# Sketched attention and a rational MoE layer on one core: the last tokens leave PSUM in two column halves

## The chip, the cores and the metric

The kernel runs on one core of one Trainium2 chip, as one program. The time is the device time of one execution in microseconds; the medians here are over repeated runs of the same program. Beside that, one execution was recorded by the hardware profiler; all rows quoted below come from that one, and their times count from the first instruction of its span.

A core has five engines that matter here: TensorE (PE in the profile, with its weight loads as PEld), VectorE (DVE), ScalarE (ACT), GpSimd (POOL) and SyncE (SP), which mostly issues transfers. SP and ScalarE each have a queue of their own for transfers (q1 and q10 in the profile), and the transfers are carried out by 16 DMA engines.

## The reference: what is computed

Four batches of four heads, 1,088 tokens each, head size 32. Queries and keys go through two small sketches, whose outer product gives 64 features per token; from these a linear attention is computed. Its output, 4,352 tokens of 128 numbers, goes through a layer of 2,048 hidden units with a rational activation:

```python
def phi(x):
    a = np.einsum('rd,bhsd->bhsr', S1, x)
    b = np.einsum('rd,bhsd->bhsr', S2, x)
    return np.einsum('bhsi,bhsj->bhsij', a, b).reshape(*x.shape[:-1], r * r)
q_p, k_p = (phi(q), phi(k))
kv = np.einsum('bhsf,bhsd->bhfd', k_p, v)
num = np.einsum('bhsf,bhfd->bhsd', q_p, kv)
den = np.einsum('bhsf,bhf->bhs', q_p, np.sum(k_p, axis=2))[..., None] + 1e-06
...
h = x @ w_in
P = a[0] + a[1] * h + a[2] * h2 + a[3] * h3
Q = 1.0 + np.abs(b[0]) * np.abs(h) + np.abs(b[1]) * h2
out = (P / (Q + 1e-06)) @ w_out
```

The result is 4,352 x 128 in float32, token by token: batch b has rows b x 1,088 to b x 1,088 + 1,087.

## The kernel before, in words

Of each batch 1,024 tokens are cut into two chunks of 512, the first chunk of all into 128 and 384. The 64 tokens that each batch has left over, 4 x 64 = 256, form one last chunk, number 9. Each chunk goes through the same steps: the attention gives its tokens, transposed, in the tile xT; the 16 blocks of the hidden layer (128 units each) are multiplied in groups, the activation is computed on VectorE and ScalarE with some sums done by accumulating transfers from GpSimd's queue, and the products with w_out are summed in one PSUM tile, out_ps (`project`).

For chunks 0 to 8 the sum stands there with the model dimension on the partitions; it is copied to SBUF, transposed by TensorE, copied by ScalarE into the tile oT (`oT_evac`, L906) and stored by SP (`store_main`, L981). The last chunk is summed by token (`BY_TOKEN`): its matmuls (L886) take 128 tokens as the weights, so out_ps has tokens on the partitions and no transpose is needed. Columns 0 to 127 of out_ps hold the left-over tokens of batches 0 and 1 (64 partitions each), columns 128 to 255 those of batches 2 and 3. One copy by ScalarE (`o_tokens`, L962) brings all 256 columns to oT, and `store_rem` (L985 to L989) issues two stores, one on SP's and one on ScalarE's queue: store i takes the partitions 64 i to 64 i + 63 with both column halves, that is the batches i and i + 2.

The kernel lists its steps through `plan.add`, each with an engine, an estimated length, the steps that it follows and the buffers that it takes and gives. The order in which the steps are issued is not planned at run time: the list `ORDER` at the head names the steps by number, and `Plan.issue` runs through it. Each engine works through its instructions in that order and waits for the others by counters; which waits an instruction gets follows from the tiles that it reads and writes. The stores of all chunks go through a tile oT with two buffers.

Of the kernel before, what the change touches and what calls it, by code (L numbers as in the profile page):

```python
# [15 lines left out]
ACT = mybir.ActivationFunctionType  # L16
# [39 lines left out]


class Plan:
# [66 lines left out]
def kernel(  # L125
# [13 lines left out]
    nc = tc.nc  # L139
    B, H, S, D = q.shape  # L140
    R = S1.shape[0]
    n_tok, d_model = out.shape
# [4 lines left out]
    MAIN = J * 128  # L147
    REM = S - MAIN
# [7 lines left out]
    BP = B // 2  # L156
# [26 lines left out]
    plan = Plan(BUFS)  # L183
    T = {}

    def tile_of(pool, name, shape, dtype):
        return pool.tile(shape, dtype, name=name, bufs=BUFS[name])
# [45 lines left out]
    def load_small(eng, i):  # L233
        s = (S1, S2)[i]
        QUEUE[eng].dma_start(out=SR[:, i, :],
                             in_=bass.AP(tensor=s.tensor, offset=s.offset, ap=[[0, 128 // R], [D, R], [1, D]]))

    def load_ab(eng):
        for dst, src in ((b_sb, moe_b), (a_sb, moe_a)):
            QUEUE[eng].dma_start(out=dst, in_=bass.AP(tensor=src.tensor, offset=src.offset,  # L240
                                                      ap=[[0, 128]] + list(src.ap)))
# [34 lines left out]
    i = plan.add("POOL", 1500, lambda: load_small("POOL", 1), rank=-99.9, name="load S2")  # L276
# [20 lines left out]
    for b in range(2, B):  # L297
        for i, (name, go) in enumerate(mains(b)):
            ld[name, b] = load("SP", go, 512, NP if name == "v" else 1, rank=-70 + i,
                               take=["v_aug" if name == "v" else "kq"])  # L300
# [69 lines left out]
    i = plan.add("POOL", 1350, lambda: load_ab("POOL"), after=[c_pool], rank=-98.9, name="load ab")  # L370
# [235 lines left out]
    def lab(n):  # L606
        return n - 1 if n > 1 else ("0", "0b")[n]
# [179 lines left out]
    def add_group(g, G):  # L787
        W, fis, n, how = G["W"], G["fis"], G["n"], G["how"]
# [26 lines left out]
        def take(kind):  # L815
            return [] if packed else [KINDS[kind][0]]

        def got(kind):
            return [T[kind, "got", n]] if packed else []

        def used(step, *kinds):
            if packed:
                for kind in kinds:
                    T[kind, "used", n].append(step)
            return step

        def give(*kinds):
            return [] if packed else [KINDS[kind][0] for kind in kinds]
# [41 lines left out]
        def mul(out, in0, in1):  # L870
            return lambda: nc.vector.tensor_mul(out=out(), in0=in0(), in1=in1())  # L871
# [38 lines left out]
        for s, nsub in subs:  # L910
            at = s * W // CW if W > B * REM or not by_token else s
            hm = plan.add("PE", 858 * nsub * W // 512, lambda s=s, w=nsub: h_mm(s, w), after=[G["x_step"], ld["wi"]], rank=g - 1.45,
                          take=["h_ps"], give=["xT"] if final and (s, nsub) == subs[-1] else [], name=f"h {g},{at}")
# [3 lines left out]
                                take=take("t") if s == 0 else [], give=["h_ps"], name=f"hev {g},{at}"))  # L917
# [3 lines left out]
        def add_up(name, dst, src, after, rank, give=()):  # L921
            if name[1] not in how:
                return plan.add("DVE", tt, lambda: nc.vector.tensor_add(out=dst(), in0=dst(), in1=src()), after=after,
                                rank=rank, give=give, name=f"{name} {g}")

            def f():
                nc.gpsimd.dma_start(out=dst(), in_=src(), accum_op=AX.add, max_dma_last_dim=GW)  # L927
            p = plan.add("POOL", 1900, f, after=after, rank=rank, name=f"{name} {g}")
            return plan.add("DMA", -(-gw // 2048) * 2048 * 1.43 if gw > 1024 else gw * 1.43, lambda: None, after=[p], rank=rank, give=give, lag=900, name=f"{name} land {g}")
# [10 lines left out]
        p = plan.add("DVE", ts + 121, odd, after=[sp, c_a] + got("y"), rank=g - 0.3, take=take("y"), name=f"odd {g}")  # L940
        p = used(plan.add("DVE", tt, mul(y, y, ht), after=[p, ab], rank=g - 0.3, give=give("t"), name=f"oddt {g}"), "t")
# [3 lines left out]
        if z:  # L945
            rt = plan.add("PE", len(fis) * pw, lambda: project("u", w_out_0, first, False),
                          after=[e, rt] + c_w0[:1 + (fis[-1] >= NF // 2)], rank=g + 0.45, take=["out_ps"] if first else [], name=f"pr {g}")
            used(rt, "u")
        p = used(add_up("+P", y, sq, [p, v, dq0], g - 0.3, give=give("sq")), "sq")
        p = used(plan.add("DVE", tt, mul(y, y, u), after=[p, e], rank=g + 0.55, give=[] if z else give("u"), name=f"n5 {g}"), "u")  # L950
        o = plan.add("PE", len(fis) * pw, lambda: project("y", w_out_b, first and not z, final), after=[p, rt] + c_w[:1 + (fis[-1] >= NF // 2)], rank=g + 0.56,
                     take=["out_ps"] if first and not z else [], give=give("y"), name=f"py {g}")
# [6 lines left out]
        if final and by_token:  # L959
            def o_tokens():  # L960
                T["oT", n] = tile_of(moe, "oT", [128, JC, d_model], FP)
                nc.scalar.copy(out=T["oT", n][:, :W // 128, :],  # L962
                               in_=T["o", n][:, :W].rearrange("p (n d) -> p n d", d=d_model))

            t = plan.add("ACT", 32 + W * 109 // 128, o_tokens, after=[o], rank=g + 0.57, take=["oT"], give=["out_ps"],
                         name=f"otev {lab(n)}")
            t = plan.add("SP", 650, lambda: G["store"](T["oT", n]), after=[t], rank=g + 0.6, name=f"store {lab(n)}")
            plan.add("ST", 1, lambda: None, after=[t], rank=g + 0.6, give=["oT"], name=f"stored {lab(n)}")
        elif final:
            ev = 32 + W * 109 // 128  # L970
            o = plan.add("ACT", ev, o_evac, after=[o], rank=g + 0.56, take=["o_sb"], give=["out_ps"], name=f"oev {lab(n)}")
            t = plan.add("PE", 110 * (W // 128), o_transposes, after=[o], rank=g + 0.57, take=["w_ps"], give=["o_sb"],
                         name=f"otr {lab(n)}")
            t = plan.add("ACT", ev, oT_evac, after=[t], rank=g + 0.57, take=["oT"], give=["w_ps"], name=f"otev {lab(n)}")
            t = plan.add("SP", 650, lambda: G["store"](T["oT", n]), after=[t], rank=g + 0.6, name=f"store {lab(n)}")
            plan.add("ST", 1, lambda: None, after=[t], rank=g + 0.6, give=["oT"], lag=700, name=f"stored {lab(n)}")
        return o

    def store_main(b, c, j0, nj):
        def f(oT):  # L980
            nc.sync.dma_start(  # L981
                out=out[b * S:b * S + MAIN, :].rearrange("(p j) d -> p j d", j=J)[:, c * JC + j0:c * JC + j0 + nj, :], in_=oT[:, :nj])
        return f

    def store_rem(oT):  # L985
        for i, eng in enumerate((nc.sync, nc.scalar)):
            eng.dma_start(out=bass.AP(tensor=out.tensor, offset=out.offset + (i * S + MAIN) * d_model,
                                      ap=[[d_model, REM], [2 * S * d_model, BP], [1, d_model]]),
                          in_=oT[i * REM:(i + 1) * REM, :BP, :])  # L989

    chunks = [(b, c, 0, JC) for b in range(B) for c in range(NCH)]
    chunks[0:1] = [(0, 0, 0, HEAD), (0, 0, HEAD, JC - HEAD)]
# [2 lines left out]
    for n in range(len(chunks) + 1):  # L995
# [4 lines left out]
        for z in sizes:  # L1000
            groups.append(dict(n=n, W=B * REM if rem else chunks[n][3] * 128, fis=list(range(f0, f0 + z)),
                               store=store_rem if rem else store_main(*chunks[n])))
# [6 lines left out]
    for n in range(len(chunks) + 1):  # L1009

        rank = first_of[n] - 2.6
        if n < len(chunks):
# [5 lines left out]
            def srcs(b=b, c=c, j0=j0, nj=nj):  # L1018
# [13 lines left out]
                give=["kq"] if c == NCH - 1 else [], early=early, pair=c if b > 0 else None)  # L1032
# [57 lines left out]
```

## Time and profile before

| what | us |
|---|---|
| median of 3 runs | 246.57 (246.38 to 246.75) |
| the profiled execution | 246.79 |
| its span, first to last instruction | 244.8 |
| busy in the span: PE, DVE, ACT | 237.0, 223.8, 219.4 |
| last copy out of PSUM (L962) | 0.37, from 240.86 |
| last two stores (L987) issued | 241.26 |

The page of the profile gives busy times of each engine, the chain of work that ended last (followed back from the last instruction: what released it, and what released that), and groups of instructions by line. The timeline lists instructions with their start and length; `<-PE out_ps` in brackets says what ended the wait before one. The DMA view lists, for a stretch of time, the share of the 16 DMA engines that were busy in 40 equal slices (a digit is tenths, 9 is 90% or more), the packets of each queue with the share of the stretch that they took on 16 engines, and the transfers issued in it with size and time from issue to landing.

### The profile page before, as it was taken

Reading aid. Unit: us, or ns where it says so; the run is one execution under the profiler, and the core shown is the slowest. Engines: PE = TensorE matmul, PEld = TensorE weight load, DVE = VectorE, ACT = ScalarE, POOL = GpSimd, SP = SyncE. Lnnn points to the kernel's source line nnn. Section 1 sums busy time; section 2 is a strip of 40 time slices with the busy share of each in tenths; the row PEclk is TensorE's granted clock in tenths of the full one; section 3 lists DMA queues with packets and bytes.
Section 4 is the critical chain, followed back from the end, with each engine's and each line's share of the span. In section 5 each row is a group of like instructions: output and inputs, shape, how many; then the busy total and the mean of one; then the engine's idle time right before and its main releaser. Section 6 shows DMA issues by size and latency. Waiting matters only on the chain.

```text
span 244.8 us, 3043 instructions
## 1 busy us (share of the span) xinstructions
PE 237.0 (97%) x1138; PEld 137.0 (56%) x1138; DVE 223.8 (91%) x241; ACT 219.4 (90%) x198; POOL 50.1 (20%) x70
## 2 busy tenths in 40 slices
PE   8999999999999999999999999999999999999983
PEld 4888676655566555554554655344344444655452
DVE  0759969999999999999999999999999998999992
ACT  3337998998899979999999999999999999999993
POOL 7800020104021505030121420212211113111100
PEclk9999999999999999999999999999999999999999
DMA  6996716668959799989999899999999999999912
GB/s 165 277 319 170 255 22 111 166 135 196 188 99 185 126 183 181 188 158 191 205 173 184 151 212 187 187 209 183 189 189 215 185 175 181 203 190 179 194 43 67
DMA packets 22207, 42.96 MB, mean 175 GB/s; under 512 B 5537, under 2 KB 12721, under 8 KB 22065
## 3 DMA queue, kind: packets, MB, share of 16 engines
q0 software_dynamic: 8544, 31.74, 72.5%
q1 hardware_dynamic: 13360, 10.95, 14.9%
q8 instruction: 9, 0.15, 0.2%
q10 hardware_dynamic: 288, 0.08, 0.2%
q14 instruction: 6, 0.04, 0.0%
HBM read 8.82 MB, written 2.23 MB: 45 GB/s over the span
## 4 chain that ended last, share of the span: by engine, by line
PE 81%; DVE 8%; DMA 4%; ACT 4%; issue 2%; SPq 0%; DVEq 0%; ACTq 0%
PE h_ps L834 44%; PE out_ps L891 11%; PE w_ps L501 7%; DVE y L871 4%; PE w_ps L688 3%; PE w_ps L630 3%; PE w_ps L464 3%; PE w_ps L676 3%; DMA u<-lin 3%; PE w_ps L620 2%; ACT L L875 2%; DMA kq<-in_k_dram 2%; ACT u L878 2%; PE w_ps L455 1%; DVE lin L861 1%
## 5 line engine op out<-in xcount | busy, mean ns | idle before, releaser
L834 PE MATMUL h_ps<-xT,w_in_sb 128*128 128x512 f32 (+3 forms) x320 | 127.4, 534 | 0.0
L834 PEld LDWEIGHTS h_ps<-xT,w_in_sb 128*128 128x128 f32 x320 | 55.2, 190 | 42.1 <-issue 32.4
L875 ACT ACTIVATE L<-u,kappa 128x4096 f32<-128x4096 bf16 (+6 forms) x23 | 65.9, 2866 | 0.2 <-DMA u<-lin 0.2
L878 ACT ACTIVATE u<-L 128x4096 bf16<-128x4096 f32 (+6 forms) x23 | 63.7, 2769 | 0.1
L841 ACT CAST hb<-h_ps 128x1024 bf16<-128x1024 f32 (+3 forms) x52 | 52.1, 1022 | 5.1 <-PE h_ps L834 4.9
L927 POOL DMA_DIRECT2D u<-lin x17 | 21.1, 1241 | 115.8 <-DVE u L853 42.2
L871 DVE TENSOR_TENSOR y<-y,u 128x4096 bf16<-128x4096 bf16 (+6 forms) x23 | 39.6, 1727 | 1.1 <-ACT u L878 1.1
L871 DVE TENSOR_TENSOR y<-y,hb 128x4096 bf16<-128x4096 bf16 (+6 forms) x23 | 39.6, 1728 | 0.1
L861 DVE TENSOR_TENSOR lin<-hb 128x4096 bf16<-128x4096 bf16 (+6 forms) x22 | 38.0, 1728 | 0.7 <-ACT hb L841 0.6
L927 POOL DMA_DIRECT2D y<-lin x15 | 20.6, 1370 | 61.6 <-DVE lin L868 19.8
L891 PE MATMUL out_ps<-y,w_out_b 128*128 128x512 bf16 (+2 forms) x144 | 30.6, 355 | 0.9 <-DVE y L871 0.9
L865 DVE TENSOR_SCALAR y<-lin,a_t 128x4096 bf16<-128x4096 bf16 (+6 forms) x23 | 25.0, 1089 | 1.1 <-PE out_ps L891 0.9
L891 PEld LDWEIGHTS <-w_out_b 128*128 128x128 bf16 x144 | 13.3, 98 | 20.2 <-issue 7.9
L853 DVE TENSOR_SCALAR u<-hb 128x4096 int16<-128x4096 int16 (+6 forms) x23 | 21.6, 941 | 0.3 <-ACT hb L841 0.2
L891 PE MATMUL out_ps<-u,w_out 128*128 128x512 bf16 x64 | 15.1, 379 | 0.0
L841 DVE CAST hb<-h_ps 128x1024 bf16<-128x1024 f32 x12 | 14.6, 1214 | 0.0
L501 PEld LDWEIGHTS w_ps<-v_aug,k_p 128*128 128x128 f32 x112 | 13.4, 192 | 1.3 <-issue 1.0
L501 PE MATMUL w_ps<-v_aug,k_p 128*128 128x96 f32 x112 | 13.7, 274 | 0.0
L484 DVE TENSOR_TENSOR k_p<-ab 128x1024 f32<-128x1024 f32 x7 | 8.6, 1231 | 3.9 <-ACT q_pT L682 2.3
L891 PEld LDWEIGHTS <-w_out 128*128 128x128 bf16 x64 | 6.2, 98 | 8.4 <-issue 2.3
L868 DVE TENSOR_SCALAR lin<-lin,a_t 128x4096 bf16<-128x4096 bf16 (+3 forms) x11 | 10.9, 989 | 0.0
L676 PEld LDWEIGHTS w_ps<-ident,q_p 128*128 128x128 f32 x66 | 8.1, 141 | 5.0 <-issue 4.6
(121 smaller groups left out, 230.5 us busy)
## 6 DMA issues: line engine op xcount, KB each, us to landing
u<-lin POOLq DMA_DIRECT2D x14, 1024.0 KB, 9.4
y<-lin POOLq DMA_DIRECT2D x13, 1024.0 KB, 9.8
v_aug<-in_v_dram SPq DMA_DIRECT2D x8, 256.0 KB, 5.0
out_dram<-oT SPq DMA_DIRECT2D x7, 256.0 KB, 4.7
kq<-in_k_dram SPq DMA_DIRECT2D x3, 512.0 KB, 4.3
kq<-in_q_dram SPq DMA_DIRECT2D x3, 512.0 KB, 6.3
u<-lin POOLq DMA_DIRECT2D x2, 768.0 KB, 8.0
w_in_sb<-in_moe_w_in_dram SPq DMA_DIRECT2D x1, 1024.0 KB, 5.6
```

The source lines that it names most:

```text
L501: nc.tensor.matmul(kv_of((hp,))[:, 0], lhsT=lhs(hp), rhs=rhs(hp), start=(first and hp == hps[0]), stop=final, skip_group_check=True)
L676: nc.tensor.transpose(T["qpTp", n, hp][:, i * 128:(i + 1) * 128], in_=qp[:, i, hp * 128:(hp + 1) * 128], identity=ident)
L834: nc.tensor.matmul(T["h", g, s][:, i * step:i * step + W], lhsT=w_in_sb[:, fi * 128:(fi + 1) * 128], rhs=T["xT", n][:, :W], start=True, st ...
L841: copy(out=T["t", g][:, s * W:(s + nsub) * W], in_=T["h", g, s][:, :nsub * W])
L853: nc.vector.tensor_scalar(out=u().bitcast(mybir.dt.int16), in0=ht().bitcast(mybir.dt.int16), scalar1=0x7FFF, scalar2=None, op0=AX.bitwise_and)
L861: nc.vector.tensor_mul(out=sq(), in0=ht(), in1=ht())
L865: nc.vector.tensor_scalar(out=y(), in0=sq(), scalar1=a_t[:, 3:4], scalar2=a_t[:, 1:2], op0=AX.mult, op1=AX.add)
L871: return lambda: nc.vector.tensor_mul(out=out(), in0=in0(), in1=in1())
L875: nc.scalar.activation(out=T["L", g][:, :gw], in_=u(), func=ACT.Ln, bias=1.0 + 1e-6, scale=kappa[:, 2:3])
L878: nc.scalar.activation(out=u(), in_=T["L", g][:, :gw], func=ACT.Exp, scale=-1.0)
L891: nc.tensor.matmul(T["o", n][:, :W], lhsT=w[:, fi, :], rhs=T[src, g][:, i * W:(i + 1) * W], start=(start and i == 0), stop=(stop and i == ...
L927: nc.gpsimd.dma_start(out=dst(), in_=src(), accum_op=AX.add, max_dma_last_dim=GW)
```

## The change

The 256 columns of the last chunk are copied out of PSUM by two engines: columns 0 to 127 by ScalarE, columns 128 to 255 by VectorE. The two stores are divided the same way: SP stores the first half (batches 0 and 1, all 128 partitions), ScalarE's queue the second (batches 2 and 3). One step more is in the plan, so the numbers behind it rise by one, and the new step (800) stands right behind ScalarE's copy (799) in the order.

```diff
-     794, 798, 792, 679, 780, 790, 795, 793, 799, 796, 731, 800, 732, 801, 797]
+     794, 798, 792, 679, 780, 790, 795, 793, 799, 800, 796, 731, 801, 732, 802, 797]
...
             def o_tokens():
                 T["oT", n] = tile_of(moe, "oT", [128, JC, d_model], FP)
-                nc.scalar.copy(out=T["oT", n][:, :W // 128, :],
-                               in_=T["o", n][:, :W].rearrange("p (n d) -> p n d", d=d_model))
-
-            t = plan.add("ACT", 32 + W * 109 // 128, o_tokens, after=[o], rank=g + 0.57, take=["oT"], give=["out_ps"],
-                         name=f"otev {lab(n)}")
-            t = plan.add("SP", 650, lambda: G["store"](T["oT", n]), after=[t], rank=g + 0.6, name=f"store {lab(n)}")
+                nc.scalar.copy(out=T["oT", n][:, :W // 256, :],
+                               in_=T["o", n][:, :W // 2].rearrange("p (n d) -> p n d", d=d_model))
+
+            def o_batches():
+                nc.vector.tensor_copy(out=T["oT", n][:, W // 256:W // 128, :],
+                                      in_=T["o", n][:, W // 2:W].rearrange("p (n d) -> p n d", d=d_model))
+
+            t = plan.add("ACT", 32 + W * 109 // 256, o_tokens, after=[o], rank=g + 0.57, take=["oT"], name=f"otev {lab(n)}")
+            t2 = plan.add("DVE", 72 + W // 2, o_batches, after=[o], rank=g + 0.57, give=["out_ps"], name=f"otev2 {lab(n)}")
+            t = plan.add("SP", 650, lambda: G["store"](T["oT", n]), after=[t, t2], rank=g + 0.6, name=f"store {lab(n)}")
...
     def store_rem(oT):
-        for i, eng in enumerate((nc.sync, nc.scalar)):
-            eng.dma_start(out=bass.AP(tensor=out.tensor, offset=out.offset + (i * S + MAIN) * d_model,
-                                      ap=[[d_model, REM], [2 * S * d_model, BP], [1, d_model]]),
-                          in_=oT[i * REM:(i + 1) * REM, :BP, :])
+        for k, eng in enumerate((nc.sync, nc.scalar)):
+            eng.dma_start(out=bass.AP(tensor=out.tensor, offset=out.offset + (2 * k * S + MAIN) * d_model,
+                                      ap=[[S * d_model, 2], [d_model, REM], [1, d_model]]), in_=oT[:, k])
```

The list in `ap` gives step and count of each dimension of the DRAM side, outermost first: before 64 rows, 2 batches, 128 numbers; after 2 batches, 64 rows, 128 numbers. On the side of SBUF the partitions are outermost: 64 before, 128 after.

14 rows, old and new, of the table ORDER are left out of this document.

## The prediction

> **What bounds the kernel now.** I read the page first: its busy times, and the shares of the chain that ended last.
>
> ```profile
> span 244.8 us, 3043 instructions
> ...
> PE 237.0 (97%) x1138; PEld 137.0 (56%) x1138; DVE 223.8 (91%) x241; ACT 219.4 (90%) x198; POOL 50.1 (20%) x70
> ...
> PE 81%; DVE 8%; DMA 4%; ACT 4%; issue 2%; SPq 0%; DVEq 0%; ACTq 0%
> ```
>
> Three engines are busy nine tenths of the span, and TensorE carries 81% of the chain. None of that is touched: up to the last matmul both kernels issue the same instructions in the same order on every engine. So the question is only what follows that matmul. The timeline of the end:
>
> ```profile
> 240.19 0.29 DVE L871 TENSOR_TENSOR y<-y,u 128x256 bf16<-128x256 bf16 x1 [0.29 <-ACT u L878]
> 240.54 0.28 PE L886 MATMUL out_ps<-w_out_b,y 128*128 128x128 bf16 x2
> 240.66 0.33 SPq L981 DMA_DIRECT2D out_dram<-oT  x1
> 240.86 0.37 ACT L962 COPY oT<-out_ps 128x256 f32<-128x256 f32 x1 [0.23 <-PE out_ps L886]
> 241.26 0.65 SPq L987 DMA_DIRECT2D out_dram<-oT  x1
> 241.26 0.69 ACTq L987 DMA_DIRECT2D out_dram<-oT  x1
> ```
>
> The last copy runs from 240.86 to 241.23, and the two last stores are issued 0.03 us later, together. Next the DMA view of 241.2 to 244.9 (the digits are the busy share of the 16 DMA engines in slices of 0.0925 us):
>
> ```profile
> DMA  0006999999600016999996100000000000000000
> ...
> DMA packets 432, 0.39 MB, mean 106 GB/s; under 512 B 48, under 2 KB 304, under 8 KB 432
> ...
> out_dram<-oT SPq DMA_DIRECT2D x1, 64.0 KB, 2.1
> out_dram<-oT ACTq DMA_DIRECT2D x1, 64.0 KB, 2.4
> ```
>
> Three stores fall in it, each of 144 packets (432/3): 128 of data and 16 of less than 512 B, the number of DMA engines. The digits 9 say that nearly all engines work at once. ScalarE's store lands last, at 241.26 + 2.4 = 243.66; from there to the end of the span are 244.8 - 243.66 = 1.14 us, which I keep. So the end is: copy 0.37, hop 0.03, store 2.4, closing 1.14. All the change can win by quicker copies is a few tenths; what a store costs is the large term.
>
> **The change, part by part.**
>
> *The copies.* ScalarE copies 128 columns instead of 256, VectorE the other 128:
>
> ```profile
> L896 ACT COPY o_sb<-out_ps 128x128 f32<-128x128 f32 x1 | 0.3, 277 | 0.0
> L721 DVE TENSOR_TENSOR o_sb<-w_ps,den_e 128x128 f32<-128x128 f32 x1 | 0.3, 281 | 0.0
> L566 DVE TENSOR_TENSOR z_bd<-w_ps,mask 128x16 f32<-128x16 f32 x2 | 0.3, 168 | 0.0
> ```
>
> ScalarE: 0.28 for 0.37, so SP's store can be issued at 240.86 + 0.28 + 0.03 = 241.17, 0.09 earlier. VectorE's copy has no row. By the 128x128 multiply out of PSUM it is 0.28; the 128x16 row bounds it below at 0.17. I take 0.28. But the two do not run side by side. They write one tile, oT, and in the changed program the last wait of VectorE's copy is for ScalarE's counter at the value of ScalarE's copy. VectorE answers ScalarE within 0.03 us (its 240.19 above, after a ScalarE instruction that ran from 239.74 for 0.42):
>
> ```profile
> 239.74 0.42 ACT L878 ACTIVATE u<-L 128x256 bf16<-128x256 f32 x1
> ```
>
> So it copies from 241.17 to 241.45, and ScalarE's store is issued at 241.48, 0.22 later than now. Behind that wait ScalarE has nothing but the end of the program; behind the copy VectorE has nothing. VectorE's copy also waits for earlier stores out of the same buffer. The youngest of them was issued at 236.40 and took 4.2, so it is in at 240.6, before the last matmul ends, and costs nothing:
>
> ```profile
> 236.40 0.33 SPq L981 DMA_DIRECT2D out_dram<-oT  x1
> ```
>
> ```profile
> out_dram<-oT SPq DMA_DIRECT2D x1, 256.0 KB, 4.2
> ```
>
> *The stores.* Before, store i takes 64 partitions and two batches: 64 x 2 runs of 128 floats, and the outermost dimension is 64 in SBUF and 64 in DRAM. After, store k takes all 128 partitions of one half: 128 runs in SBUF, but 2 (batches) x 64 x 128 in DRAM. Runs, bytes and their length (512 B) stay; what changes is that the DRAM side's outermost dimension falls from 64 to 2. That matters if a store is dealt out to the DMA engines by its outermost dimension. What the rows say for it: the shape goes to the queue with its dimensions, since the issue of the two-dimensional stores takes 0.65 and 0.69, that of the plain one 0.33; and a store whose two sides both begin with 64 uses all sixteen engines. With 128 on one side and 2 on the other, the only equal cut that fits both outermost dimensions is in two. No store or load of the trace has a dimension below 16 outermost, so it cannot show the case itself; the bounds are sixteen engines (nothing changes) and two.
>
> The Trainium skill, page "DMA: Bandwidth & Descriptors", section "Why a DMA increments its semaphore by 16 and not by 1", states the rule outright: the engine count is the largest number up to 16 that divides the outermost dimension of both patterns, and the lowest-numbered engines are taken. By it each of these stores gets two engines, and both stores the same two. The trace agrees for 64 (16 small packets a store); no run here shows a 2.
>
> The price by rows. One packet of 512 B, from a dense stretch of the first loads (2.6 to 3.0, all packets of 512 B), from the last two stores (242.45 to 243.45), from the first of these while crowded (242.45 to 242.86), and packets of 2,048 B of the store before them (241.2 to 242.4):
>
> ```profile
> DMA packets 255, 0.13 MB, mean 326 GB/s; under 512 B 0, under 2 KB 255, under 8 KB 255
> ...
> q1 hardware_dynamic: 255, 0.13, 112.9%
> ```
>
> ```profile
> DMA  0000433789889979979989999989762310000000
> ...
> q1 hardware_dynamic: 144, 0.07, 33.0%
> q10 hardware_dynamic: 144, 0.07, 27.9%
> ```
>
> ```profile
> DMA packets 100, 0.05 MB, mean 124 GB/s; under 512 B 1, under 2 KB 100, under 8 KB 100
> ...
> q1 hardware_dynamic: 100, 0.05, 60.9%
> ```
>
> ```profile
> DMA  0000000008359799799399398795996841200000
> ...
> q1 hardware_dynamic: 144, 0.26, 58.2%
> ```
>
> Share x 16 engines x stretch / packets: 1.129 x 16 x 400 / 255 = 28.3 ns; in the last stores 36.7 and 31.0 ns; crowded 0.609 x 16 x 410 / 100 = 40.0; and 0.582 x 16 x 1200 / 144 = 77.6 ns for 2,048 B, a quarter of which, 19.4, no 512 B packet should beat. I take 28.3, the row with the most packets and no mixture; 19.4 and 40.0 are the ends.
>
> The start: in slices of 25 ns the first packet of the two stores falls in the fifth, 242.55, that is 1.29 after the issue at 241.26; the last ends near 243.30, 0.36 before the landing. The plain store's first packet comes at 241.2 + 9 x 0.03 = 241.47, 0.81 after its issue. I take 1.29 (same store, two dimensions), with 0.81 as the low end.
>
> The sum, both stores on the same two engines: SP's store issued 241.17, first packet 242.46; ScalarE's packets arrive about 1.6 after 241.48, at 243.1 (the stretch up to 242.86, above, holds packets of SP's queue q1 alone, none of ScalarE's q10), while SP's 64 packets per engine still run (64 x 28.3 = 1.81, to 244.27). So each engine works through without a gap: 128 x 28.3 = 3.62, to 246.08, landing 246.44, against 243.66: +2.78. VectorE's 0.22 is hidden behind SP's packets; without that cover it would add 0.22. The profiled execution took 246.79 for its span of 244.8 (1.99 around it); it would take 249.57. The median of the runs shown is 0.22 lower, 246.57, so the forecast is 249.35. Its own range: with 19.4 and 0.81 the landing is 241.17 + 0.81 + 2.48 + 0.36 = 244.82, +1.16, 247.73; with 40.0, 242.46 + 5.12 + 0.36 = 247.94, +4.28, 250.85.
>
> **The rivals.**
>
> *Two engines a store, but not the same two.* For it: the two stores sit in two queues (q1 and q10). Against it: in the view of the last two stores both queues keep the same sixteen engines busy, so neither owns any. ScalarE's store then lands at 241.48 + 1.60 + 1.81 + 0.36 = 245.25: +1.59, 248.16 (247.4 with a start of 0.81).
>
> *All sixteen engines still: not slower.* The store could be cut by its 128 partitions alone, or by its 128 packets. For it: every store of the trace, whatever its shape, has its 16 small packets. Then only the copies count: ScalarE's store is issued 0.22 later; if issuing apart brings its 0.69 down to the plain store's 0.33 it wins back up to 0.36. Between -0.14 and +0.22; at 246.7, no change. It decides the matter from 8 engines on: 16 packets each of 28.3 ns are then 0.45 for a store, about what the stores take now.
>
> *The copies do run side by side, and the issues no longer crowd.* ScalarE's store issued at 241.17, landing after the 2.0 of a plain store: 243.2, -0.46, 246.1. Against it stands the wait on ScalarE's counter.
>
> ```profile
> out_dram<-oT SPq DMA_DIRECT2D x1, 256.0 KB, 2.0
> ```
>
> **How the numbers follow.** Same two engines 0.72: the shape reaches the queue with its dimensions, and two is the only cut of both outermost ones. Different pairs 0.10. Sixteen engines 0.16, since no row shows a small outermost dimension. Side by side 0.02. A measurement of this kernel tells 0.2%, about 0.5 us, from no change. The first two are slower (0.82), the third is within it, the last just about faster. The prediction is 249.35. The range goes from the second case's 247.4 to the first one's 250.85; it leaves out the third and fourth, 0.18, and the thin ends.
>
> **What would show it.** VectorE's copy starts about 0.03 after ScalarE's copy ends, not beside it. SP's store is issued near 241.2 and ScalarE's near 241.5. The DMA digits after 242.4 stand at 1 (two engines of sixteen) instead of 9, for some 3.6 us; the stores take about 5 us to land; each has fewer than 16 small packets. Wrong would be digits of 7 to 9 and a landing after 2 us (sixteen engines), digits at 2 (two pairs), or packets that in a stream of two engines do not take 28 ns each.

## The result, and the profile after

The changed kernel takes 249.24 us (median of 4 runs, 248.84 to 249.54) against 246.63 (246.38 to 246.75) for the kernel before, run beside it: ratio 1.0104, 95% interval 1.0092 to 1.0116. It is 2.61 us slower; 249.35 was forecast. The profiled execution took 249.54 for a span of 247.5.

The end of the changed kernel, from its timeline (start, length, engine, line):

```profile
240.71 0.28 PE L886 MATMUL out_ps<-w_out_b,y 128*128 128x128 bf16 x2
240.83 0.33 SPq L985 DMA_DIRECT2D out_dram<-oT  x1
241.04 0.27 ACT L962 COPY oT<-out_ps 128x128 f32<-128x128 f32 x1 [0.23 <-PE out_ps L886]
241.33 0.68 SPq L991 DMA_DIRECT2D out_dram<-oT  x1
241.34 0.29 DVE L966 COPY oT<-out_ps 128x128 f32<-128x128 f32 x1 [0.68 <-ACT oT L962]
241.66 1.15 ACTq L991 DMA_DIRECT2D out_dram<-oT  x1
```

The last matmul ends at 240.99, 0.17 later than in the profile of before; that is ahead of anything the change touches. So all comparisons below count from the end of the last matmul to the end of the span: 4.01 us before, 6.49 after. The bracket on VectorE's row says that it waited for ScalarE's copy: it began at 241.34, when that had ended. Nothing ran side by side.

The DMA view of 241.2 to 247.5 (digits: busy share of the 16 DMA engines in slices of 0.16 us):

```profile
DMA  0017999301111111111111111111110000000000
...
DMA packets 404, 0.39 MB, mean 62 GB/s; under 512 B 20, under 2 KB 276, under 8 KB 404
...
q1 hardware_dynamic: 274, 0.33, 15.1%
q10 hardware_dynamic: 130, 0.07, 3.5%
```

Before, two stretches of digits up to 9 followed each other. Now the first stretch, the store of the chunk before, is as it was, and then comes a row of ones. There are 20 packets of less than 512 B where there were 48. The earlier store has its 16, which leaves 4 for the two last ones, two each. Two engines of sixteen carry the two stores. The stages of this stretch, from a view by windows (PE, PEld, DVE, ACT, POOL busy; granted clock; DMA share; GB/s):

```profile
241.30:242.60 1.30, 0.00 (x0) 0.00 (x0) 0.29 (x1) 0.00 (x1) 0.00 (x0) 1.00 0.54 202
242.60:246.00 3.40, 0.00 (x0) 0.00 (x0) 0.00 (x0) 0.00 (x0) 0.00 (x0) 0.69 0.14 39
246.00:247.50 1.50, 0.00 (x0) 0.00 (x0) 0.00 (x0) 0.00 (x0) 0.00 (x0) 0.50 0.00 0
```

For 3.40 us the core does nothing but move the 128 KB of the two last stores at 39 GB/s, with 0.14 of its DMA engines; 2/16 is 0.125. And in the view of waits (us in total, times, longest) SP, which closes the program, waited 1.5 us for stores before (241.0 to 244.8) and 4.1 after (241.0 to 247.5):

```profile
SPq L1085 <- DMA out_dram<-oT: 1.5, 2, 1.0
```

```profile
SPq L1088 <- DMA out_dram<-oT: 4.1, 2, 3.4
```

### The profile page after: what moved, and what is told of

It reads as the page before. It is cut to its first block, busy times and chain, and to the rows that moved or that the text cites. A ratio compares the mean times of both kernels' runs of the same rounds, so it can differ in the third digit from the quotient of the medians.

```text
span 247.5 us, 3035 instructions
## 1 busy us (share of the span) xinstructions
PE 236.2 (95%) x1127; PEld 137.1 (55%) x1138; DVE 224.0 (91%) x242; ACT 219.2 (89%) x198; POOL 50.1 (20%) x70
## 4 chain that ended last, share of the span: by engine, by line
PE 81%; DVE 8%; ACT 4%; DMA 3%; issue 2%; DVEq 0%; ACTq 0%
PE h_ps L834 44%; PE out_ps L891 11%; PE w_ps L501 7%; DVE y L871 4%; PE w_ps L688 3%; PE w_ps L464 3%; PE w_ps L630 3%; PE w_ps L676 3%; DMA u<-lin 3%; PE w_ps L620 2%; ACT L L875 2%; ACT u L878 2%; PE w_ps L455 1%; PE out_ps L360 1%; DVE lin L861 1%
## 5 line engine op out<-in xcount | busy, mean ns | idle before, releaser
L891 PE MATMUL out_ps<-y,w_out_b 128*128 128x512 bf16 (+2 forms) x136 | 30.0, 354 | 1.3 <-DVE y L871 0.9
L891 PE MATMUL out_ps<-u,w_out 128*128 128x512 bf16 x61 | 14.6, 379 | 0.1
L682 ACT COPY q_pT<-w_ps 128x512 f32<-128x512 f32 (+2 forms) x18 | 10.8, 598 | 0.1
```

What stands on the lines that cost most here:

```text
L891: nc.tensor.matmul(T["o", n][:, :W], lhsT=w[:, fi, :], rhs=T[src, g][:, i * W:(i + 1) * W], start=(start and i == 0), stop=(stop and i == ...
```

## The experiments

The theory: a store is dealt out to as many DMA engines as the outermost dimension of its narrower side allows, and two engines for two stores are the whole cost. The rivals: the copies and their wait cost the time; or the place of the bytes (128 partitions, or the rows of DRAM that follow each other) does.

Each run was timed against the kernel before on the same chip. In the table "stretch" is from the end of the last matmul to the end of the span of the profiled execution, and "small" counts the packets under 512 B that belong to the last stores.

| kernel | ratio to before (95%) | stretch, us | small packets / stores |
|---|---|---|---|
| before | 1 | 4.01 | 32 / 2 |
| the change | 1.0104 (1.0092 to 1.0116) | 6.49 | 4 / 2 |
| copies alone | 1.0014 (1.0003 to 1.0025) | 4.26 | 32 / 2 |
| stores alone | 1.0104 (1.0082 to 1.0126) | 6.71 | 4 / 2 |
| four stores, 64 outermost | 0.9999 (0.9985 to 1.0013) | 4.16 | 64 / 4 |
| four stores, 8 outermost | 1.0028 (1.0016 to 1.0041) | 4.89 | 32 / 4 |
| four stores, 4 outermost | 1.0042 (1.0029 to 1.0056) | 4.96 | 16 / 4 |
| four stores, 2 outermost | 1.0098 (1.0078 to 1.0118) | 6.53 | 8 / 4 |
| 2 outermost on SP's queue alone | 1.0048 (1.0030 to 1.0066) | 5.09 | 34 / 3 |
| 2 outermost on ScalarE's queue alone | 1.0063 (1.0047 to 1.0079) | 5.38 | 34 / 3 |
| four stores, two SBUF tiles | 1.0014 (1.0002 to 1.0026) | 4.18 | 64 / 4 |
| four stores, two PSUM tiles | 1.0007 (0.9996 to 1.0018) | 4.08 | 64 / 4 |
| stores of before, two PSUM tiles | 0.9994 (0.9984 to 1.0003) | 4.01 | 32 / 2 |

### The copies alone

```diff
 # the change, with the stores of before
-        for k, eng in enumerate((nc.sync, nc.scalar)):
-            eng.dma_start(out=bass.AP(tensor=out.tensor, offset=out.offset + (2 * k * S + MAIN) * d_model,
-                                      ap=[[S * d_model, 2], [d_model, REM], [1, d_model]]), in_=oT[:, k])
+        for i, eng in enumerate((nc.sync, nc.scalar)):
+            eng.dma_start(out=bass.AP(tensor=out.tensor, offset=out.offset + (i * S + MAIN) * d_model,
+                                      ap=[[d_model, REM], [2 * S * d_model, BP], [1, d_model]]),
+                          in_=oT[i * REM:(i + 1) * REM, :BP, :])
```

> The column halves are copied by ScalarE and VectorE as in the change, the two stores are those of before (64 partitions, outermost dimension 64 on both sides). Theory, the engines that a store gets: sixteen again, 32 small packets for the two stores, and only the copies' chain counts, +0.2 to +0.3 us against before, 246.85. Rival, the copies and VectorE's wait are what costs: as slow as the change, 249.2.

247.19 us, ratio 1.0014. That is 0.34 above the expected time, but the kernel before took 246.81 beside it, 0.2 more than the 246.6 from which the expectation counts. The stretch is 4.26, 0.25 longer than before, as expected. The copies follow each other and both stores wait for the second one:

```profile
241.36 0.27 ACT L962 COPY oT<-out_ps 128x128 f32<-128x128 f32 x1 [0.23 <-PE out_ps L886]
241.66 0.29 DVE L966 COPY oT<-out_ps 128x128 f32<-128x128 f32 x1 [0.68 <-ACT oT L962]
241.98 0.66 SPq L991 DMA_DIRECT2D out_dram<-oT  x1
241.98 0.69 ACTq L991 DMA_DIRECT2D out_dram<-oT  x1
```

So the split copies, with these stores, cost 0.25 us instead of saving any. The other 2.2 us of the change's 2.48 are not theirs.

### The stores alone

```diff
 # before, with the stores of the change
-        for i, eng in enumerate((nc.sync, nc.scalar)):
-            eng.dma_start(out=bass.AP(tensor=out.tensor, offset=out.offset + (i * S + MAIN) * d_model,
-                                      ap=[[d_model, REM], [2 * S * d_model, BP], [1, d_model]]),
-                          in_=oT[i * REM:(i + 1) * REM, :BP, :])
+        for k, eng in enumerate((nc.sync, nc.scalar)):
+            eng.dma_start(out=bass.AP(tensor=out.tensor, offset=out.offset + (2 * k * S + MAIN) * d_model,
+                                      ap=[[S * d_model, 2], [d_model, REM], [1, d_model]]), in_=oT[:, k])
```

> ScalarE alone copies all 256 columns as before, the two stores are divided by column halves as in the change (DRAM side 2 x 64 x 128). Theory, the engines that a store gets: two completion packets a store, digits of 1, both stores issued 0.1 us later than SP's in the change, 249.2 to 249.4. Rival, the copies cost: 246.6, as before.

249.18 us, ratio 1.0104: the time of the change itself (249.24), without VectorE's copy. The DMA view of 241.8 to 246.0 of this kernel has 260 packets, 2 x 128 and four small ones:

```profile
DMA  0101111111110110111111111111111111000000
...
DMA packets 260, 0.13 MB, mean 31 GB/s; under 512 B 4, under 2 KB 260, under 8 KB 260
```

The shape of the stores is the cause. With it the copies count for nothing: in this kernel ScalarE's store is issued 0.44 us after the last matmul, in the change 0.67, and the change is not slower for it. In the profiled executions the change's stretch is even 0.22 shorter. With the stores alone the first data packet leaves 0.09 later, since SP's store waits for the copy of all 256 columns, and the packets take 3.53 us instead of 3.40, with two slices of digit 0 in the middle of the ones. Why they pause there is not shown.

### Four stores, one per batch: 64, 8, 4 and 2 outermost

```diff
-        for k, eng in enumerate((nc.sync, nc.scalar)):
-            eng.dma_start(out=bass.AP(..., ap=[[S * d_model, 2], [d_model, REM], [1, d_model]]), in_=oT[:, k])
+        for i in range(2):
+            for k, eng in enumerate((nc.sync, nc.scalar)):
+                eng.dma_start(out=bass.AP(tensor=out.tensor, offset=out.offset + ((2 * k + i) * S + MAIN) * d_model,
+                                          ap=[[d_model, REM], [1, d_model]]), in_=oT[i * REM:(i + 1) * REM, k])
 # with m of 2, 4 or 8 outermost instead:
+                                          ap=[[d_model, m], [m * d_model, REM // m], [1, d_model]])
```

> Copies as in the change; each half is stored in two stores, one per batch, 64 partitions to 64 rows in a row, two stores on each queue. Theory, the engines that a store gets: sixteen for each of the four; +0.2 for the copies and some tenths for the second issue on ScalarE's queue, 246.8 to 247.2. Rival, it is the place of the bytes in DRAM or the 128 partitions of a half that makes the store slow: 248 to 249.

> As the four stores per batch, same bytes, same 64 rows each, but the DRAM side is written as 2 x 32 rows, the even rows and then the odd ones (the rows of a batch land in another order, so the left-over rows of the output are permuted). Theory, the engines that a store gets: two, the same for all four stores, 4 x 32 packets of 28.3 ns each, 3.62 us, as slow as the change: 249.2 to 249.6. Rival, place in DRAM or partitions: like the four stores with 64 rows outermost.

> As the four stores per batch with 2 x 32 rows, but 4 x 16 rows on the DRAM side (rows permuted within a batch). Theory, the engines that a store gets: four, the same four for all stores; 4 x 16 packets of 27 to 28 ns each, 1.8 us instead of 3.5, so 1.7 less than with two engines: 247.3 to 247.6, unless the issues take longer than that. Rival, it is the second dimension on the DRAM side as such that is slow, whatever its count: 249.0, as with two.

> The same with 8 x 8 rows (permuted within a batch). Theory, the engines that a store gets: eight; 4 x 8 packets each, 0.9 us, less than the four issues take, so the time of the four stores with 64 rows outermost, 246.8 to 247.1. Rival, the second dimension as such: 249.0.

246.76, 249.03, 247.74 and 247.48 us for 64, 2, 4 and 8. The DMA views of the four, each over its last stores (64: 241.96 to 243.8; 2: 242.0 to 246.5; 4: 242.3 to 245.5; 8: 242.1 to 245.5):

```profile
DMA packets 320, 0.13 MB, mean 71 GB/s; under 512 B 64, under 2 KB 320, under 8 KB 320
```

```profile
DMA  0111111111111111111111111111111000000000
...
DMA packets 264, 0.13 MB, mean 29 GB/s; under 512 B 8, under 2 KB 264, under 8 KB 264
```

```profile
DMA  0132223222222222200122222000000000000000
...
DMA packets 272, 0.13 MB, mean 41 GB/s; under 512 B 16, under 2 KB 272, under 8 KB 272
```

```profile
DMA  0354313442454100000445100000000000000000
...
DMA packets 288, 0.13 MB, mean 39 GB/s; under 512 B 32, under 2 KB 288, under 8 KB 288
```

Four stores of the same bytes from the same partitions to the same rows of DRAM have 16, 2, 4 and 8 small packets each: one per engine, and as many engines as the outermost count, up to sixteen. The digits stand at 1, 2 and 4 or 5, which is 2, 4 and 8 of sixteen. That shuts out the partitions and the place in DRAM, and a second dimension as such.

The kernel with two engines came out 0.2 us below what was expected, those with four and eight 0.1 and 0.4 above. For these last two the gap in their digits shows why: the engines are idle between the third and the fourth store. ScalarE's first issue takes 1.23 us with eight engines and 0.52 with sixteen. The timelines with eight engines and with sixteen:

```profile
240.86 1.45 SPq L992 DMA_DIRECT2D out_dram<-oT  x2
241.19 1.89 ACTq L992 DMA_DIRECT2D out_dram<-oT  x2
```

```profile
240.80 1.18 SPq L992 DMA_DIRECT2D out_dram<-oT  x2
241.13 1.16 ACTq L992 DMA_DIRECT2D out_dram<-oT  x2
```

Two issues on ScalarE's queue take 1.89 us instead of 1.16, so the last store starts 0.7 later; the stretch differs by 0.73. With eight engines it is the issue, not the engines, that sets the end; with four the gap is shorter, but there too the engines stand idle before the last store.

### One store with two engines, the other half with sixteen

```diff
 # on SP's queue: its half as in the change, ScalarE's as two stores of 64 rows; and the mirror image
-        for k, eng in enumerate((nc.sync, nc.scalar)):
-            eng.dma_start(out=..., in_=oT[:, k])
+        nc.sync.dma_start(out=bass.AP(..., ap=[[S * d_model, 2], [d_model, REM], [1, d_model]]), in_=oT[:, 0])
+        for i in range(2):
+            nc.scalar.dma_start(out=bass.AP(..., ap=[[d_model, REM], [1, d_model]]), in_=oT[i * REM:(i + 1) * REM, 1])
```

> Copies as in the change; the first half is stored by SP as in the change (2 x 64 x 128), the second half by ScalarE's queue in two stores of 64 rows in a row. Theory, the engines that a store gets: the two engines work off 64 packets instead of 128, 1.8 us, and the sixteen-engine stores pass beside them; the stretch from the last matmul to the end of the span is 1.61 + 1.81 + 0.3 + 1.17 = 4.9 us, 0.9 more than before: 247.5. Rival, the two stores do not share engines and each is slow by itself: 249.2, as the change.

> The mirror image: SP stores the first half in two stores of 64 rows, ScalarE's queue the second half as in the change (2 x 64 x 128). In the change ScalarE's issue takes 1.15 us and its first packet leaves 2.5 us after the issue begins. If the packets came so late because the two engines were still busy with SP's, this store starts about 1.4 us after its issue and the stretch from the last matmul to the end is 0.66 + 1.4 + 1.81 + 0.32 + 1.17 = 5.4 us, 248.0. If it is the long issue on ScalarE that delays them, 0.66 + 2.5 + 1.81 + 0.32 + 1.17 = 6.5 us, 249.2, as the change.

248.03 and 248.41 us, 0.5 and 0.4 above the expected times; the kernel before took 246.82 beside them, which is 0.2 of that. The stretches are 5.09 and 5.38, where 4.9 and 5.4 were expected and 6.5 if each such store were slow on its own. One of the two costs 1.1 to 1.4 us, both together 2.5: they add up because they share their two engines. The mirror image also settles why ScalarE's packets left so late in the change (3.16 us after the last matmul): there its issue is as long (1.13 us), but its first packet leaves 1.3 us after the issue begins. In the change SP's packets were in the way, not the issue.

The stretch of the first of the two missed by 0.2, and its issue rows show where. They give the time to landing of the sixteen-engine stores, beside the two-engine one on SP's queue and without it (the four stores, 64 outermost):

```profile
out_dram<-oT ACTq DMA_DIRECT2D x2, 32.0 KB, 2.9
```

```profile
out_dram<-oT ACTq DMA_DIRECT2D x2, 32.0 KB, 1.9
```

A store on sixteen engines is in when the last of them has finished, and two of them still had the other store's packets to carry. The completions in the trace show the two: of each sixteen-engine store fourteen of its sixteen come together, by 3.13 us after the last matmul for the first store and 3.33 for the second, and the other two at 3.66 and 3.68, at 4.02 and 4.05. SP's own store was in at 3.87, 0.15 later than in the sum. I had expected them to pass beside.

### Why VectorE waits: two SBUF tiles, two PSUM tiles

```diff
 # two SBUF tiles (four stores of 64 rows)
-                nc.vector.tensor_copy(out=T["oT", n][:, W // 256:W // 128, :],
+                T["oT2", n] = moe.tile([128, 1, d_model], FP, name="oT2", bufs=1)
+                nc.vector.tensor_copy(out=T["oT2", n],
 ...
 # two PSUM tiles, one oT (with four stores of 64 rows, and with the stores of before)
                 T["o", n] = ops.tile([128, CW], FP, name="out_ps", bufs=1)
+                if by_token:
+                    T["o2", n] = tile_of(aps, "w_ps", [128, CW], FP)
 ...
-                        nc.tensor.matmul(T["o", n][:, k * 128:(k + 1) * 128],
+                        nc.tensor.matmul((T["o2", n] if k else T["o", n])[:, :128],
-                                         rhs=w[:, fi, :], start=(start and i == 0 and k == 0),
+                                         rhs=w[:, fi, :], start=(start and i == 0),
 ...
-                                      in_=T["o", n][:, W // 2:W]...
+                                      in_=T["o2", n][:, :W // 2]...
```

> One PSUM tile as in the change, but the two column halves are copied into two SBUF tiles; four stores of 64 rows each. If VectorE waits for ScalarE because both write the tile oT, its copy now starts beside ScalarE's and the stretch from the last matmul to the end falls from 4.17 to about 4.1. If it waits because both read one PSUM tile, the row of VectorE's copy still shows the wait for ScalarE's copy and the stretch stays 4.17; either way 246.7 to 246.9.

> Four stores of 64 rows each, one tile oT, but the second column half is summed in a PSUM tile of its own (another bank). Two theories of VectorE's wait for ScalarE's copy. If it comes from both copies writing oT, the wait stays and the time is that of the four stores, 246.8. If it comes from both reading one PSUM tile, VectorE's copy starts beside ScalarE's, ScalarE's two stores are issued 0.3 us earlier, and the stretch from the last matmul to the end of the span shortens from 4.17 to about 3.9 us, against 4.01 before: 246.4 to 246.6, hardly to be told from before.

> The second column half in a PSUM tile of its own, copies by ScalarE and VectorE, the two stores of before (64 partitions, both halves). With the copies side by side the stores are issued 0.08 us earlier than before: the stretch from the last matmul to the end of the span 3.93 us against 4.01, 246.6 to 246.7, the same as before. If the copies still follow each other, 4.27 as with the copies alone, 246.9 to 247.1.

VectorE's copy with two SBUF tiles, and both copies with two PSUM tiles, from the timelines:

```profile
241.17 0.29 DVE L967 COPY oT<-out_ps 128x128 f32<-128x128 f32 x1 [0.68 <-ACT oT L962]
```

```profile
241.34 0.27 ACT L964 COPY oT<-out_ps 128x128 f32<-128x128 f32 x1 [0.17 <-PE out_ps L888]
241.40 0.29 DVE L968 COPY oT<-w_ps 128x128 f32<-128x128 f32 x1 [0.38 <-PE w_ps L888]
```

With an oT of its own VectorE still waits for ScalarE's copy (247.02 us, stretch 4.18). With a PSUM tile of its own it waits for TensorE and runs beside ScalarE. The wait comes from both reading one PSUM tile, not from both writing one SBUF tile. It is a wait that stands in the program; no run leaves it out, so none shows whether the chip would need it.

What side by side is worth: 246.69 us with the four stores (ratio 1.0007, 0.9996 to 1.0018; the stretch 4.08 instead of 4.16, not the 3.9 expected), and 246.46 with the stores of before (0.9994, 0.9984 to 1.0003; the stretch 4.01, as before, not 3.93). With two ScalarE stores in a row the second one's issue sets the end. Both began about 0.3 us earlier, but the second took 0.82 us instead of 0.61, so it ended only 0.08 earlier. With the stores of before both issues wait for the later of the copies and began only 0.02 to 0.04 earlier than before. No version of this kind can be told from the kernel before, and none beats it.

## Why the prediction was right

*The number of engines* was the step that decided, and it held: two engines a store, both stores on the same two. The experiments with 64, 8, 4 and 2 outermost show it as a rule for the counts that were tried, where the trace of before could only say that 64 gives sixteen. The Trainium skill, page "DMA: Bandwidth & Descriptors", section "Why a DMA increments its semaphore by 16 and not by 1", states it for any count: the largest number up to 16 that divides the outermost counts of both sides. These runs agree where they tried it: 16, 8, 4 and 2 small packets a store. Only the DRAM side's count was varied, and only in powers of two; what a count like 10 or 100 would give, no run here shows.

*The sum*, counted from the last matmul, against the trace after: first packet 1.64 forecast, 1.6 measured; 128 packets in turn 3.62 forecast, 3.40 measured, 26.6 ns each instead of 28.3; from there to the landing 0.36 and 0.32; closing 1.14 and 1.17. Together 6.8 against 6.49, a rise of 2.48 instead of 2.78. The packets' price was the term that was too high. It is the mean time of one packet, while what adds up is the distance from one packet to the next. In the dense stretch that it came from the two differ, as its share of 112.9% says: packets of one engine overlap, and 0.4 us x 16 / 255 gives one every 25.1 ns. The same two figures from the change, 242.6 to 246.0:

```profile
DMA packets 260, 0.13 MB, mean 39 GB/s; under 512 B 4, under 2 KB 260, under 8 KB 260
...
q1 hardware_dynamic: 130, 0.07, 7.3%
q10 hardware_dynamic: 130, 0.07, 6.5%
```

The shares add up to 13.8% where two engines are 12.5%: 28.9 ns for a packet, but one data packet every 26.6 on each engine.

The sum also had ScalarE's first packet at 2.28 us after the last matmul (243.1), 1.2 before SP's last would end. It came at 3.16, only 0.6 before SP's last ended, because SP's packets were in its way (the mirror image above). The digits stand at 1 all the while, so the two engines had work and the sum lost nothing by it.

That 249.35 lies 0.11 from the measured 249.24 is partly luck. The rise in the traces was 0.30 smaller than forecast; the rise of the medians, 2.61, holds 0.13 that the two stretches do not show, and the kernel before measured 0.06 more beside the change than in the forecast.

*The copies.* SP's store at 0.35 after the last matmul (0.34 measured), VectorE's copy 0.28 (0.29), ScalarE's store 0.66 (0.67): each held. That VectorE's part is hidden behind SP's packets held too: with the stores alone, where nothing waits for VectorE, the median is the same. What failed is the reason that was given, that "they write one tile, oT": the runs showed that the shared PSUM tile is what makes VectorE wait. The number did not hang on it.

*The rivals.* Two pairs of engines: no, the two stores add up. Sixteen engines: no, two small packets a store. Side by side: no; and where it was made so, with four stores and with the stores of before, it was worth nothing measurable, not the 0.46 that the prediction gave it. "It decides the matter from 8 engines on" held for the engines but not for the time: with eight, in four stores, the kernel is 0.28% slower (0.16 to 0.41), because ScalarE's second issue waits behind its longer first. Two stores on eight engines each were not run.

## What to carry to other kernels

When a store is cut anew, read its address lists from the outside in: the smallest outermost count, here that of the DRAM side, and not the bytes, the rows or the partitions, decided how many DMA engines carried it, and the same bytes as four plain stores of 64 rows took no more time than before. At the end of this program nothing hides a store, so it is the first thing to count there; a copy of 0.37 us, shared between two engines, could not have paid for the 2.48 that the stores cost. Two engines that read one PSUM tile take turns in this kernel, and a split of such a copy needs a PSUM tile for each part.

## What the runs showed that was not expected

ScalarE's first issue of a store with fewer than sixteen engines takes 1.13 to 1.37 us; SP's first takes 0.67 to 0.76, and ScalarE's own first with sixteen 0.51 to 0.69. With two outermost ScalarE's second issue was back at 0.52. The first packets are not held up by it (1.3 us after the issue begins on ScalarE's queue in the mirror image), but the next instruction of that queue is. The runs do not tell why; whether it comes once per program or after each pause was not tried.

A store on sixteen engines that passes beside one on two lands up to about an us later than alone (2.9 instead of 1.9 in the median of two): the narrow store makes two of its sixteen engines late. The mirror image shows it too: of the second of SP's stores fourteen completions are in by 3.18 us after the last matmul, the other two at 3.70 and 3.74.
